# Three squares of the first batch on GpSimd, one relu more on VectorE, and the loads between them, in an attention and feed-forward kernel

## The chip, the cores and the metric

The kernel runs on one core of a Trainium2 chip. The metric is the device time of one execution in microseconds (us). The kernel before the change takes 399.31 us, the median of three runs (399.07 to 399.46).

## What is computed

The inputs are q, k and v (8 batches, 12 heads, 448 positions, 64 per head) and three weight matrices, all fp32.

```python
scores = scale * np.matmul(q, k.transpose(0, 1, 3, 2))
attn = np.maximum(scores, 0.0) ** 2 / S
x = np.matmul(attn, v)                        # then heads side by side: (3584, 768)
gate = np.maximum(x @ w_gate, 0.0)            # w_gate, w_val: (768, 1536)
out = (gate * (x @ w_val)) @ w_out            # w_out: (1536, 768)
```

So attention has no softmax: each score goes through a relu and is squared. The feed-forward part is a gated one. The kernel works in bf16 with fp32 sums and puts the scale factors into a later step.

## The kernel before, in words

**Tiles of a batch.** For each batch the scores are made in 21 tiles (`tile_of`, L244): 3 groups of four heads (`qd`) by 7 blocks of 64 positions. A tile is four matmuls that fill two PSUM banks, 128 x 896 fp32. `relu2` (L232 to L235) then takes the tile out of PSUM with a relu on ScalarE into a bf16 buffer `r_sb` (L234, from a pool of four), and squares it on VectorE into `attn` (L235). The seven squares of a group are the moving operand of 28 value matmuls (`value_passes`, L253), which add up over the seven in two other banks (banks 6 and 7, called `both`). VectorE copies their result to `x` (L663 and L669 for the first two groups; ScalarE at L685 for the third), and the two halves are swapped over partitions by `exchange` (L260; VectorE's share is L266, ScalarE's L264).

**The units of the feed-forward part.** A unit (`gv_unit`) makes 128 columns of the hidden layer of one batch in 12 steps called passes. Each pass multiplies a piece of `x` by weights from `gv_sb`, which is loaded in six chunks of 256 columns, two units each, a gate half and a value half per chunk (`load_gv`, L162 to L165).

**The order of the work.** Nothing is planned at run time. Every instruction is pinned in the order in which the program names it, so each engine's queue is as written. While batch b's attention is done, the units of batch b-1 fill TensorE. The first batch has nothing before it, and `first_batch` (L620) writes its order out by hand: tiles 0 to 16 in a loop, with relus and squares two tiles behind (`scored`, L635, takes the oldest tile from the list `todo`), then tiles 17 to 20 with the first passes of units 0, 1 and 2 among them. PSUM is short: tiles 0 to 16 take turns in three pairs of banks, so tile n can be made only when the relu of tile n-3 has read its banks. Tiles 17 and 19 take banks 2 and 3, tiles 18 and 20 banks 0 and 1; units 0, 1 and 2 add up in banks 4, 2 and 0. Ahead of it, `second_by_dve` (L638) is used once, at n = 2: VectorE does the relu of the second tile on the list (L641) and its square (L643), while the first goes through `scored`.

**The loads.** GpSimd issues nearly all loads (`dma_in`, L115), in the order of L604 to L616: k, q and v of batch 0, chunks 0 and 1 of gv, k and q of batch 1 (`load_qk(1)`, L612), and then chunks 2 and 3, v of batch 1 and chunk 4 (L613 to L616: 2 + 2 + 4 + 2 loads). After `first_batch`, at L774 to L776, it issues k of batch 2, chunk 5 and q of batch 2. GpSimd also makes copies of one element in later batches (`hold`, L703, and `hold_unit`, L699) that only wait for something and keep what stands behind them back.

Of the kernel before, what the change touches and what calls it, by code (L numbers as in the profile page):

```python
# [12 lines left out]
ALU = mybir.AluOpType  # L13
# [3 lines left out]
def kernel(  # L17
# [22 lines left out]
    nc = tc.nc  # L40
# [25 lines left out]
    HALVES = [(c, slice(c * 64, c * 64 + 64)) for c in range(2)]  # L66

    def pin(ins):
        return tc.keep_in_program_order(ins)
# [45 lines left out]
    def dma_in(o, i):  # L115
        pin(nc.gpsimd.dma_start(out=o, in_=i))  # L116
# [23 lines left out]
    def load_qk(b, h0=0, h1=H):  # L140
        load_nat(kn_b[natural(b)], k, b, h0, h1)
        load_nat(qn_b[natural(b)], q, b, h0, h1)

    def load_v(b):
        for c, p in HALVES:
            if b == 0:
                src = v[b].rearrange("(g c h) s d -> c h g s d", c=2, h=2)[c]
                dst = v_b[b % NB][p].rearrange("p (g h) i d -> p h g i d", h=2)
                parts = [(dst[:, h2], src[h2]) for h2 in range(2)]
            else:  # L150
                parts = [(v_b[b % NB][p], v[b, c * HP:c * HP + HP])]
            for dst, src in parts:
                dma_in(dst[:, :, 0:4, :], src[:, 0:256, :].rearrange("g (j i) d -> j g i d", i=4))
                dma_in(dst[:, :, 4:7, :], src[:, 256:448, :].rearrange("g (j i) d -> j g i d", i=3))
# [4 lines left out]
    gv_sb = [const.tile([128, H, n], BF16, name=f"gv{i}") for i, (_, n) in enumerate(CHUNKS)]  # L159
    wo_sb = [const.tile([128, KF // 2, d_model], BF16, name=f"wo{i}") for i in range(2)]  # L160

    def load_gv(c):  # L162
        for (_, p), src in zip(HALVES, (moe_w_gate, moe_w_val)):
            f0, n = CHUNKS[c]
            dma_in(gv_sb[c][p], src.rearrange("(h p) f -> p h f", p=64)[:, :, f0:f0 + n])  # L165

# [35 lines left out]
    def transposes(b, hp, bank):  # L202

        ps = bank.bitcast(BF16).rearrange("p (t c) -> p t c", t=2)
        for t, nat in enumerate((kn_b[b % NB], qn_b[b % NB])):
            for i in range(4):
                for h2, half in HALVES:
                    pin(nc.tensor.transpose(ps[half, t, i * 128:i * 128 + 128], nat[:, 2 * hp + h2, i, :], ident))  # L208
        pin(nc.vector.tensor_copy(T_b[b % NB][:, :, hp, :], ps[:, :, 0:S]))  # L209

    def first_transposes(numbers):

        for n, (hp, t) in zip(numbers, ((0, 0), (0, 1), (1, 0), (1, 1))):
            ps = banks[:, n, :].bitcast(BF16)
            for i in range(4):
                for h2, half in HALVES:
                    pin(nc.tensor.transpose(ps[half, i * 128:i * 128 + 128],  # L217
                                            (kn_b, qn_b)[t][0][:, 2 * hp + h2, i, :], ident))
            o = T_b[0][:, t, hp, :]
            if (hp, t) == (1, 0):  # L220
                pin(nc.scalar.activation(o, ps[:, 0:S], AF.Copy))
            else:
                pin(nc.vector.tensor_copy(o, ps[:, 0:S]))
# [5 lines left out]
                transposes(b, pair_of(b, 2 * qd + c), ps[:, c, :])  # L229
        sc_later()  # L230

    def relu2(src, dst):  # L232
        r = rpool.tile([128, 2, S], BF16, name="r_sb")
        pin(nc.scalar.activation(r, src, AF.Relu))  # L234
        pin(nc.vector.tensor_tensor(dst, r, r, ALU.mult))  # L235

    attns = {}

# [5 lines left out]
    def tile_of(b, n, ps):  # L244

        qd, i = divmod(n, NC)
        T = T_b[b % NB]
        a = i * 128 if i < 4 else (i - 4) * 128 + 64
        mm4([ps[:, r, :S] for r in range(2)], lambda r, c: T[:, 0, pair_of(b, 2 * qd + c), a:a + 64],
            lambda r, c: T[:, 1, pair_of(b, 2 * qd + c), :], True, True)  # L250
        return ps[:, :, :S], attn_of(b, qd)[:, 2 * i:2 * i + 2, :]

    def value_passes(b, qd, ps, i0, i1):  # L253

        attn, v_sb = attn_of(b, qd), v_b[b % NB]
        for i in range(i0, i1):
            mm4([ps[:, r, :S] for r in range(2)], lambda r, c: v_sb[:, 2 * qd + c, i, :],
                lambda r, c: attn[:, 2 * i + c, :], i == 0, i == NC - 1)

    def exchange(b, qd, first=None):  # L260
        x0, x1 = (x_of[b][e][qd] for e in range(2))
        for (c, p), (_, other) in zip(HALVES, HALVES[::-1]):
            if first is not None and c == 0:
                pin(first.activation(x1[p], x0[other], AF.Copy))  # L264
            else:
                pin(nc.vector.tensor_copy(x1[p], x0[other]))  # L266
# [19 lines left out]
    def idle_matmuls(ps, n):  # L286

        for _ in range(n):
            mm2(ps[:, :S], blank[:, 0:128], blank, True, True)
# [318 lines left out]
    load_nat(qn_b[0], q, 0, 8, H)  # L608
    load_v(0)
    load_gv(0)  # L610
    load_gv(1)
    load_qk(1)  # L612
    load_gv(2)  # L613
    load_gv(3)
    load_v(1)
    load_gv(4)  # L616

    NT = NQ * NC

    def first_batch(units):  # L620


        def passes(u, n):
            for _ in range(n):
                units[u].pop(0)()

        def bank(n):
            return banks[:, n, :]

        def tile(n, at=None):  # L630
            todo.append(tile_of(0, n, sc_first() if at is None else banks[:, at:at + 2, :]))

        todo = []

        def scored():  # L635
            relu2(*todo.pop(0))

        def second_by_dve():  # L638
            src, dst = todo.pop(1)
            r = rpool.tile([128, 2, S], BF16, name="r_sb")  # L640
            pin(nc.vector.tensor_scalar(r, src, 0.0, None, ALU.max))  # L641
            scored()
            pin(nc.vector.tensor_tensor(dst, r, r, ALU.mult))  # L643

        idle_matmuls(bank(6), 12)
        first_transposes((6, 7, 5, 4))
        idle_matmuls(bank(0), 4)
        tile(0)
        tile(1)
        both = banks[:, 6:8, :]  # L650
        for n in range(2, 17):
            tile(n)
            if n in (3, 5, 7, 9):
                hp = n // 2 + 1
                transposes(0, hp, bank(6 + hp % 2))
            if n == 12:
                value_passes(0, 0, both, 0, NC)
            if n == 2:
                second_by_dve()
            elif n > 3:  # L660
                scored()
            if n == 12:
                pin(nc.vector.tensor_copy(x_of[0][0][0], both[:, :, :S]))  # L663
        scored()
        value_passes(0, 1, both, 0, 4)
        passes(0, 2)
        tile(17, 2)
        value_passes(0, 1, both, 4, NC)
        pin(nc.vector.tensor_copy(x_of[0][0][1], both[:, :, :S]))  # L669
        scored()  # L670
        tile(18, 0)
        scored()
        tile(19, 2)
        passes(0, 2)
        scored()
        tile(20, 0)
        scored()
        value_passes(0, 2, both, 0, 4)
        scored()
        passes(1, 4)  # L680
        passes(2, 4)
        value_passes(0, 2, both, 4, NC)
        exchange(0, 0, nc.scalar)
        exchange(0, 1)
        pin(nc.scalar.activation(x_of[0][0][2], both[:, :, :S], AF.Copy))  # L685
        exchange(0, 2)
        for n in range(4):
            for u in range(2):
                passes(u, 2)

    def scores_event(b, n):
        return lambda: relu2(*tile_of(b, n, sc_later()))
# [77 lines left out]
    new_x(0)  # L770
    units = gv_units(0)
    first_batch(units)
    sc_later(), acc()
    load_nat(kn_b[natural(2)], k, 2, 0, H)  # L774
    load_gv(5)
    load_nat(qn_b[natural(2)], q, 2, 0, H)  # L776
    for b in range(1, B - 1):
# [8 lines left out]
        else:  # L786
            todo = [e for e in attention if e[:2] <= ENDS[b]]
# [88 lines left out]
```

## Time and profile before

| what | before |
|---|---|
| median of three runs | 399.31 us |
| the profiled execution | 399.31 us |
| its span, first to last instruction | 397.5 us |
| TensorE (PE) busy | 387.9 us, 98% |
| VectorE (DVE) busy | 302.2 us, 76% |
| ScalarE (ACT) busy | 244.3 us, 61% |
| GpSimd (POOL) busy | 97.1 us, 24% |
| granted TensorE clock | 1.000 |
| relu on ScalarE (L234) | 167 times, 936 ns each in the mean |
| square on VectorE (L235) | 167 times, 622 ns each in the mean |

The profile names engines by short names: PE is TensorE, DVE VectorE, ACT ScalarE, POOL GpSimd. A line of a timeline gives start, length, engine, line of the kernel, operation, tiles (out<-in), shapes and a count; in brackets stands how long the engine was idle before and what ended that. All starts are in us from the beginning of the span. Lengths of instructions that follow each other on an engine overlap, so the distance between two starts is the better price of one. The chain of work that ended last is followed back from the last instruction: at each step to what released it.

### The profile page before, as it was taken

What the parts mean: (1) busy time and instruction counts of PE and PEld (TensorE: products, weight loads), DVE (VectorE), ACT (ScalarE), POOL (GpSimd) and SP (SyncE); (2) the same over time, 40 slices, a digit from 0 to 9 for tenths busy, and PEclk for the clock granted to TensorE, in tenths of its full rate; (3) what the DMA queues carried; (4) which work ended last, traced back from release to release, by engine and by line L of the source; (5) the groups of instructions that cost most, each with busy time, mean ns of one, the idle gap of its engine ahead of it and who ended that gap; (6) DMA issues with size and microseconds to landing.
All of it is one profiled execution on the core that took longest, in us unless ns stands there. A gap on an engine that the chain in (4) does not pass through costs nothing.

```text
span 397.5 us, 16431 instructions
## 1 busy us (share of the span) xinstructions
PE 387.9 (98%) x7304; PEld 283.5 (71%) x7304; DVE 302.2 (76%) x531; ACT 244.3 (61%) x359; POOL 97.1 (24%) x168
## 2 busy tenths in 40 slices
PE   7899999999999999999999999999999999999995
PEld 3456679977776666666677688988887766777674
DVE  5976886689944696897873578888889869997922
ACT  3973993886334776988632788899873233444231
POOL 8933300800213601503041260020003120000213
PEclk9999999999999999999999999999999999999999
DMA  9999997999945896998963498560002340000135
GB/s 153 173 197 195 196 178 115 128 207 195 139 109 167 110 157 88 160 137 112 135 159 81 136 126 108 115 79 4 2 3 62 84 139 2 3 3 2 24 94 166
DMA packets 90872, 44.17 MB, mean 111 GB/s; under 512 B 55424, under 2 KB 89792, under 8 KB 90800
## 3 DMA queue, kind: packets, MB, share of 16 engines
q0 software_dynamic: 51264, 28.83, 51.0%
q1 hardware_dynamic: 39104, 13.99, 20.5%
q8 instruction: 57, 0.93, 1.0%
q10 hardware_dynamic: 432, 0.30, 0.3%
q14 instruction: 15, 0.12, 0.1%
HBM read 47.19 MB, written 11.01 MB: 146 GB/s over the span
## 4 chain that ended last, share of the span: by engine, by line
PE 94%; ACT 2%; DVE 1%; DMA 1%; issue 1%; POOL 0%; POOLq 0%
PE ps L72 92%; ACT r_sb L234 2%; DMA qn<-in_q_dram 1%; PE ps L208 1%; DVE attn L235 0%; DVE x L669 0%; DVE r_sb L641 0%; DVE kqT L209 0%; PE ps L217 0%; ACT g_sb L330 0%; DVE attn L643 0%; POOL qn L116 0%; DVE attn L410 0%; POOLq L860 0%
## 5 line engine op out<-in xcount | busy, mean ns | idle before, releaser
L72 PE MATMUL ps<-x,gv 64*64 64x448 bf16 (+1 forms) x3336 | 197.0, 349 | 0.1
L72 PEld LDWEIGHTS <-gv 64*64 64x64 bf16 (+1 forms) x3960 | 143.1, 107 | 48.8 <-issue 1.6
L234 ACT ACTIVATE r_sb<-ps 128x896 bf16<-128x896 f32 x167 | 148.7, 936 | 16.4 <-PE ps L72 14.0
L235 DVE TENSOR_TENSOR attn<-r_sb 128x896 bf16<-128x896 bf16 x167 | 102.0, 622 | 30.8 <-ACT r_sb L234 21.9
L420 POOL DMA_DIRECT2D out_dram<-attn x63 | 33.1, 530 | 165.1 <-DVE attn L410 130.7
L72 PEld LDWEIGHTS <-hT 128*64 128x64 bf16 x1056 | 55.9, 110 | 20.9 <-issue 1.1
L72 PE MATMUL ps<-kqT 64*64 64x448 bf16 x672 | 65.7, 351 | 2.8 <-ACT r_sb L234 2.6
L406 ACT ACTIVATE attn<-ps 128x384 f32<-128x384 f32 (+1 forms) x64 | 28.8, 450 | 64.2 <-PE ps L72 63.7
L72 PE MATMUL ps<-wo,hT 128*64 128x384 bf16 (+1 forms) x720 | 54.3, 306 | 0.0
L331 DVE TENSOR_TENSOR hT<-ps,g_sb 128x448 bf16<-128x448 f32 x72 | 44.5, 619 | 8.8 <-ACT g_sb L330 8.4
L330 ACT ACTIVATE g_sb<-ps 128x448 bf16<-128x448 f32 x72 | 39.2, 546 | 16.2 <-PE ps L72 15.9
L410 DVE TENSOR_TENSOR attn<-ps,attn 128x384 f32<-128x384 f32 (+1 forms) x48 | 22.8, 503 | 32.1 <-ACT attn L406 17.4
L72 PEld LDWEIGHTS <-vn 64*64 64x64 bf16 (+1 forms) x888 | 34.7, 107 | 11.7 <-issue 1.3
L72 PE MATMUL ps<-attn,vn 64*64 64x448 bf16 x672 | 37.1, 350 | 0.1
L72 PEld LDWEIGHTS <-kqT 64*64 64x64 bf16 x672 | 25.7, 107 | 14.2 <-issue 5.0
L539 ACT ACTIVATE kqT<-ps 128x896 f32<-128x896 f32 x18 | 16.5, 918 | 25.0 <-PE ps L72 25.0
L116 POOL DMA_DIRECT2D vn<-in_v_dram x36 | 23.7, 681 | 17.6 <-DMA wo<-in_moe_w_out_dram 11.2
L72 PE MATMUL ps<-o_ring,hT 128*64 128x384 bf16 (+1 forms) x336 | 26.0, 306 | 0.0
L706 POOL COPY flag<-kqT 128x1 bf16<-128x1 bf16 x12 | 2.7, 244 | 89.8 <-DMA kqT<-kr 68.9
L543 DVE TENSOR_TENSOR kqT<-ps,kqT 128x896 f32<-128x896 f32 x18 | 19.5, 1085 | 5.9 <-PE ps L72 4.2
L266 DVE COPY x<-x 64x896 bf16<-64x896 bf16 x33 | 13.4, 405 | 2.5 <-ACT x L685 0.7
L116 POOL DMA_DIRECT2D qn<-in_q_dram x20 | 14.7, 764 | 1.3 <-POOLq L860 0.8
(103 smaller groups left out, 289.8 us busy)
## 6 DMA issues: line engine op xcount, KB each, us to landing
out_dram<-attn POOLq DMA_DIRECT2D x48, 96.0 KB, 2.5
out_dram<-attn SPq DMA_DIRECT2D x48, 96.0 KB, 2.6
kn<-in_k_dram POOLq DMA_DIRECT2D x7, 384.0 KB, 7.4
qn<-in_q_dram POOLq DMA_DIRECT2D x7, 384.0 KB, 9.5
vn<-in_v_dram POOLq DMA_DIRECT2D x14, 192.0 KB, 9.2
gv<-in_moe_w_gate_dram POOLq DMA_DIRECT2D x6, 384.0 KB, 11.8
gv<-in_moe_w_val_dram POOLq DMA_DIRECT2D x6, 384.0 KB, 11.8
wo<-in_moe_w_out_dram POOLq DMA_DIRECT2D x2, 1152.0 KB, 14.0
```

The source lines that it names most:

```text
L72: pin(nc.tensor.matmul(o, lhsT=l, rhs=r, start=start, stop=stop, skip_group_check=True))
L116: pin(nc.gpsimd.dma_start(out=o, in_=i))
L234: pin(nc.scalar.activation(r, src, AF.Relu))
L235: pin(nc.vector.tensor_tensor(dst, r, r, ALU.mult))
L266: pin(nc.vector.tensor_copy(x1[p], x0[other]))
L330: pin(nc.scalar.activation(g_sb, o[0], AF.Relu, scale=float(out_scale)))
L331: pin(nc.vector.tensor_tensor(hT[:, mf, col:col + S], o[1], g_sb, ALU.mult))
L406: pin(nc.scalar.activation(out_of(t, r, c), bank(P, t), AF.Copy))
L410: pin(nc.vector.tensor_tensor(o, bank(Q, t), o, ALU.add))
L420: pin(engines[c].dma_start(out=rows[:, c0:c1, :], in_=src))
L539: pin(nc.scalar.activation(held(n, j), both(PQ[n][0]), AF.Copy))
L543: pin(nc.vector.tensor_tensor(k, both(PQ[n][1]), k, ALU.add))
```

## The change

In the first batch, the squares of tiles 12, 16 and 19 are made on GpSimd instead of VectorE. The relu of tile 13 is made on VectorE instead of ScalarE, by a second use of `second_by_dve` at n = 14; its own square stays on VectorE. The loop's n = 15 takes no tile from the list any more, so that the list is as long afterwards as before. The ten loads of L613 to L616 move into `first_batch`: the gate half of chunk 2 stands on GpSimd between the squares of tiles 16 and 19, the other nine behind the square of tile 19. On GpSimd the order is therefore, behind q of batch 1: square of tile 12, square of tile 16, gate half of chunk 2, square of tile 19, value half of chunk 2, chunk 3, v of batch 1, chunk 4. TensorE's order is the same as before, instruction for instruction; SP's too. VectorE's is: copy L663, square 11, relu 13, square 13, square 14, square 15, copy L669, squares 17, 18 and 20.

```diff
-    def load_gv(c):
-        for (_, p), src in zip(HALVES, (moe_w_gate, moe_w_val)):
+    def load_gv(c, parts=(0, 1)):
+        for p, src in [(HALVES[n][1], (moe_w_gate, moe_w_val)[n]) for n in parts]:
...
-    def relu2(src, dst):
+    def relu2(src, dst, square=nc.vector):
         r = rpool.tile([128, 2, S], BF16, name="r_sb")
         pin(nc.scalar.activation(r, src, AF.Relu))
-        pin(nc.vector.tensor_tensor(dst, r, r, ALU.mult))
+        pin(square.tensor_tensor(dst, r, r, ALU.mult))
...
     load_qk(1)
-    load_gv(2)
-    load_gv(3)
-    load_v(1)
-    load_gv(4)
...
-        def scored():
-            relu2(*todo.pop(0))
+        def scored(square=nc.vector):
+            relu2(*todo.pop(0), square)
 
-        def second_by_dve():
+        def second_by_dve(square=nc.vector):
             src, dst = todo.pop(1)
             r = rpool.tile([128, 2, S], BF16, name="r_sb")
             pin(nc.vector.tensor_scalar(r, src, 0.0, None, ALU.max))
-            scored()
+            scored(square)
             pin(nc.vector.tensor_tensor(dst, r, r, ALU.mult))
...
             if n == 2:
                 second_by_dve()
-            elif n > 3:
+            elif n == 14:
+                second_by_dve(nc.gpsimd)
+            elif n not in (3, 15):
                 scored()
...
         pin(nc.vector.tensor_copy(x_of[0][0][1], both[:, :, :S]))
-        scored()
+        scored(nc.gpsimd)
+        load_gv(2, (0,))
         tile(18, 0)
         scored()
         tile(19, 2)
         passes(0, 2)
         scored()
         tile(20, 0)
-        scored()
+        scored(nc.gpsimd)
+        load_gv(2, (1,))
+        load_gv(3)
+        load_v(1)
+        load_gv(4)
         value_passes(0, 2, both, 0, 4)
```

## The prediction

> **What bounds the kernel now.** I read the page first (engine shares, slices), then the chain that ended last in order of time, then the timelines of the four engines from 17 to 27 us. By the page TensorE is busy 98% of the span at full clock, and by the chain nearly all of the time after 45.81 us is TensorE work in a row. Whatever the change moves lies before that, and what TensorE loses there is lost at the end.
>
> ```profile
> 16.18 2.11 PE ps L72 x40
> ...
> 18.31 1.07 ACT r_sb L234
> ...
> 19.42 2.60 PE ps L72 x44
> ...
> 22.04 1.10 DVE x L669
> ...
> 23.18 8.62 PE ps L72 x124
> ```
>
> Columns: start, length, what. One relu of ScalarE (L234, that of tile 13) ends at 19.38 and lets TensorE go on; one VectorE copy (L669) does so again at 23.14; from 23.18 TensorE runs on its own. So the change is worth what it does to those two releases. TensorE's timeline there:
>
> ```profile
> 18.61 0.38 PE L72 MATMUL ps<-kqT 64*64 64x448 bf16 x4 [0.34 <-ACT r_sb L234]
> 19.42 0.38 PE L72 MATMUL ps<-kqT 64*64 64x448 bf16 x4 [0.43 <-ACT r_sb L234]
> 19.61 0.95 PE L72 MATMUL ps<-attn,vn 64*64 64x448 bf16 x16
> 20.36 0.72 PE L72 MATMUL ps<-x,gv 64*64 64x448 bf16 x8
> 21.04 0.38 PE L72 MATMUL ps<-kqT 64*64 64x448 bf16 x4
> 21.23 0.76 PE L72 MATMUL ps<-attn,vn 64*64 64x448 bf16 x12
> ```
>
> The lines at 18.61 and 19.42 are tiles 15 and 16: each takes the banks of the tile three before it. Tile 16 waits for tile 13's relu, **the relu that the change gives to VectorE**. Spacings to use: a tile 0.19, 16 value matmuls 0.75, 12 of them 0.57, 8 pass matmuls 0.38 where nothing is waited for. VectorE and GpSimd:
>
> ```profile
> 18.00 1.08 DVE L663 CAST x<-ps 128x896 bf16<-128x896 f32 x1
> 19.01 2.76 DVE L235 TENSOR_TENSOR attn<-r_sb 128x896 bf16<-128x896 bf16 x5
> 22.04 1.09 DVE L669 CAST x<-ps 128x896 bf16<-128x896 f32 x1 [0.28 <-PE ps L72]
> 23.04 2.76 DVE L235 TENSOR_TENSOR attn<-r_sb 128x896 bf16<-128x896 bf16 x5
> ```
> ```profile
> 18.36 0.84 POOL L116 DMA_DIRECT2D gv<-in_moe_w_gate_dram  x1
> 20.75 0.75 POOL L116 DMA_DIRECT2D gv<-in_moe_w_val_dram  x1 [1.56 <-DMA gv<-in_moe_w_val_dram]
> ```
>
> VectorE has no free slot from 18.00 to 21.76: squares follow each other every 0.535 us (0.62 each, overlapped), a copy from PSUM takes 1.0 before the next may start. The engine that is given more work is full.
>
> **The change, part by part.** *Relu of tile 13.* ScalarE loses one of its relus, which start 0.80 apart, so those of tiles 14 and 15 come 0.80 earlier. VectorE gains one: 1.09, the L641 row (8.92, same shape, same line before the change). It stands behind the copy L663 and the square of tile 11. Even if nothing disturbs these, it runs from 19.01 + 0.535 = 19.54 to 20.63, and tile 16 starts at 20.66, not 19.42: 1.24 late. Part comes back: the 8 pass matmuls at 20.36 now find their weights there (the trace ends their wait in mid-group at 20.73, on a DMA of gv) and their relus done. From tile 16 to L669 takes 0.19 + 0.75 + 0.38 + 0.19 + 0.57, with 0.2 until the last matmul is through, 2.3 against 22.04 - 19.42 = 2.62. L669 is then late by about 0.9, and with it all that follows. So the relu alone costs 0.85.
>
> *The saved relu time itself* is worth almost nothing: the passes at 20.36 wait for gv until 20.73 whatever ScalarE does, and L669 hangs on them.
>
> *Three squares to GpSimd (tiles 12, 16, 19).* VectorE gives up 3 x 0.535. The trace has no such square on GpSimd. Below: 1.2, from the one-element flag copy (0.19) and the 128-element AFFINE_SELECT (0.33), by (0.33 - 0.19) x 7 + 0.19. Above: 7 x 0.33 = 2.3. VectorE's own 0.62 is a floor for both. I take **2.0**, nearer to the upper end, because a square reads two operands and AFFINE_SELECT one. The Trainium skill, GPSIMD Engine Reference, section "Performance versus the Vector engine", gives 4497 ns for a tensor_tensor of 2048 fp32 elements; scaled to 896 this is an estimate of 1.97, and the sum would be the same.
>
> *Do they run beside VectorE's squares?* This trace has rows:
>
> ```profile
> 228.18 0.63 DVE L235 TENSOR_TENSOR attn<-r_sb 128x896 bf16<-128x896 bf16 x1
> ```
> ```profile
> 228.30 0.55 POOL L701 COPY flag<-hT 128x1 bf16<-128x1 bf16 x1 [6.16 <-DVE hT L331]
> ```
> ```profile
> 130.86 0.67 DVE L235 TENSOR_TENSOR attn<-r_sb 128x896 bf16<-128x896 bf16 x1 [0.29 <-ACT r_sb L234]
> ```
> ```profile
> 130.75 0.30 POOL L706 COPY flag<-kqT 128x1 bf16<-128x1 bf16 x2
> ```
> ```profile
> 260.92 0.19 POOL L706 COPY flag<-kqT 128x1 bf16<-128x1 bf16 x1 [5.62 <-DMA kqT<-qr]
> ```
>
> A GpSimd copy of one element takes 0.19 beside a VectorE operation that reads PSUM (260.92). Begun inside a VectorE square it lasts until just past the square's end (228.30 + 0.55 against 228.18 + 0.63). Begun before one, at 130.75, it is not held, and the square is 0.04 longer than the usual 0.62 to 0.63. So a square and a GpSimd read exclude each other, and who is first goes first. I take that for the long squares too: **each GpSimd square stops VectorE's squares for its whole 2.0 us.** The Trainium skill, SBUF — State Buffer, section "Who interferes with whom", states it as a rule that speaks against this change: a VectorE instruction with two SBUF inputs and a GpSimd instruction that reads SBUF block each other for a whole instruction. By that rule the sum is the one that follows, without it the 0.85 above; the flag rows agree with it, most clearly in one direction.
>
> The sum, in order of time:
> 1. Tile 12's relu ends at 18.56; GpSimd is free (its last load ended at 18.45) and squares from 18.60 to 20.60. VectorE is in L663, from PSUM, so GpSimd is first.
> 2. Behind L663, tile 11's square waits until 20.60 and ends near 21.15. Queued behind it is tile 13's relu, 21.1 to 22.2, and for that waits TensorE: tile 16 at 22.2, **2.8 late**.
> 3. TensorE needs 2.3 to L669, which starts at 24.5 (before: 22.04) and ends at 25.6.
> 4. Tile 16's square holds GpSimd and the port from 23.95 to 25.95, mostly beside L669; tile 17's ends at 26.5. Tile 20 runs at 26.0, the first 16 value matmuls at 26.2, the 32 pass matmuls at 26.95 to 28.46 (1.5 as before).
> 5. GpSimd issues one load (0.75, to 26.70), then wants tile 19's square (relu done 26.6), meets tile 18's square on VectorE until 27.07, and works from 27.1 to 29.1. Tile 20's relu is done at 27.46, but its square waits until 29.1 and ends at 29.68.
> 6. The last 12 value matmuls: tile 18 at 28.46, tile 19 at 29.13, tile 20 at 29.71, the last issued by 29.90. Before, they began at 26.02 and were issued by 26.61: **+3.3**.
> 7. The half-swap copies L266 on VectorE, before at 25.83, now follow tile 20's square and end 0.1 behind TensorE: +0.1. TensorE's wait for qn at 32.21 shrinks by 0.06.
>
> In all +3.3. With 1.2 for a square the same steps give +1.6, with 2.31 +4.2.
>
> *The ten loads that move* (gv2, gv3, v1, gv4) and those queued behind them on GpSimd (kn, gv5, qn, first at 38.52) I cost at nothing. Each issue before waits for an older landing (20.75 above); landings come some 2 us apart, and qn of batch 1, the last load ahead of the moved ones, lands at 32.36. The moved ones now start at 25.95, 29.1 and 29.9, still ahead of that. Without this cover gv2 would be 2 us later per load; its user, unit 4, starts at 36.8 + 3.3, so 3 us of that are covered too. SP's queue is not touched.
>
> **The rivals.** (a) *No mutual hold*: VectorE's squares run beside GpSimd's. Then only the relu counts: +0.85 - 0.06, 400.1. For it: the holds seen last 0.4 at most. (b) *GpSimd always gives way*: its first square then ends at 22.9 instead of 20.6, 0.55 after the value matmuls want it; with the relu's 0.85 that is +1.4 by L669, and the later two add up to 1.5: 400.7 to 402.2. For it: the clear flag rows are all of this direction; against it, 130.86. (c) *Not slower*: there is no hold, and the 0.85 is swallowed further on. TensorE's load queue has waits of 0.4, 0.2, 0.3 and 0.4 near 45, 53, 80 and 91 us; if what ends them does not move with TensorE, they take it all: 399.3. It decides from 0.85 of such time on. Against it: the chain names L234 relus and L330 there, which follow TensorE's own tiles. (d) *Faster*: VectorE gets to tile 13's relu before 18.3; then ScalarE's 0.80 counts, but the gv landing at 20.73 leaves some 0.1: 399.2. The full VectorE row speaks against it.
>
> **How the numbers follow.** The profiled execution took 399.31 us (span 397.5, 1.8 around it), equal to the median 399.31 of three runs. Forecast: 399.31 + 3.3 = 402.6, chance 0.65, its own range 400.9 (1.2 per square) to 403.6 (2.31). (b) 0.10, (a) 0.15, (c) 0.07, (d) 0.03. The range reaches down to (a) and up to the price's upper end: 400.0 to 403.7. A change of 0.2%, 0.8 us, is about what a measurement of this kernel can tell from none; (a) lies on that bound and is split in two. Slower 0.83, same 0.14, faster 0.03.
>
> **What would show it.** GpSimd squares of 1.2 to 2.3 us at about 18.6, 24 and 27; a VectorE square begun at 19.0 that lasts some 2 us; tile 16 at 22.2, its wait ended by VectorE's relu (L637); L669 (now L667) at 24.5; the last value matmuls of the first batch at 28.5 to 30; unit 4's weights without a wait. It is wrong if the VectorE squares beside GpSimd's keep their 0.62 (then tile 16 is at 20.7), if a GpSimd square takes under 1 us, or if TensorE waits for gv after 36 us.

## The result, and the profile after

The changed kernel takes 403.54 us, the median of six runs (402.93 to 404.21), against 399.76 us for the kernel before (six runs, 399.07 to 401.48): ratio 1.0091, 95% interval 1.0072 to 1.011, so slower by 0.9%. The profiled execution has a span of 401.7 us (before 397.5). Forecast were 402.6 us and +3.3; the medians differ by 3.8, the two profiled spans by 4.2. Two of all the executions below, at a mean clock of 0.75 (512.78 us) and 0.56 (683.91 us), ran slow throughout and count in no ratio. A ratio is the recorded one; it can differ by up to 0.0012 from the quotient of the medians beside it.

The chain that ended last, in the changed kernel (start, length, what):

```profile
18.88 1.86 DVE attn L235
20.73 1.01 DVE r_sb L637
...
21.79 3.87 PE ps L72 x34
...
25.68 1.10 DVE x L667
```

Where the chain before had one relu of ScalarE, it now has a VectorE square of 1.86 us and VectorE's relu behind it; only then does TensorE go on, at 21.79. The copy of the second group (now L667) follows at 25.68, before at 22.04. The timelines of GpSimd and VectorE in the changed kernel:

```profile
18.57 1.68 POOL L235 TENSOR_TENSOR attn<-r_sb 128x896 bf16<-128x896 bf16 x1
23.48 1.68 POOL L235 TENSOR_TENSOR attn<-r_sb 128x896 bf16<-128x896 bf16 x1 [3.23 <-ACT r_sb L234]
25.10 0.80 POOL L116 DMA_DIRECT2D gv<-in_moe_w_gate_dram  x1
27.67 1.71 POOL L235 TENSOR_TENSOR attn<-r_sb 128x896 bf16<-128x896 bf16 x1 [1.77 <-ACT r_sb L234]
```
```profile
18.88 1.86 DVE L235 TENSOR_TENSOR attn<-r_sb 128x896 bf16<-128x896 bf16 x1
20.66 1.08 DVE L637 TENSOR_SCALAR r_sb<-ps 128x896 bf16<-128x896 f32 x1
28.64 1.22 DVE L235 TENSOR_TENSOR attn<-r_sb 128x896 bf16<-128x896 bf16 x1 [0.80 <-ACT r_sb L234]
29.89 3.25 DVE L266 COPY x<-x 64x896 bf16<-64x896 bf16 x5
```

A GpSimd square takes 1.68. A VectorE square that comes up while one runs (18.88, 28.64) ends 0.48 after it, though alone it takes 0.62 (GpSimd's ends at 18.57 + 1.68 = 20.25, VectorE's at 20.74). This is the hold of which the prediction speaks. TensorE's timeline:

```profile
21.79 0.59 PE L72 MATMUL ps<-kqT 64*64 64x448 bf16 x4 [2.86 <-DVE r_sb L637]
22.11 1.75 PE L72 MATMUL ps<-attn,vn 64*64 64x448 bf16 x16
...
31.88 1.31 PE L72 MATMUL ps<-x,gv 64*128 64x448 bf16 x12 [0.40 <-DVE x L266]
```

The 16 value matmuls that took 0.95 now take 1.75, and there is a new wait of 0.40 for the swap copies (`exchange`, L266, five on VectorE in this stretch). The reason of the first stands in the busy time by stretches (us, busy time and count of each engine, granted TensorE clock, DMA share, GB/s), for the changed kernel:

```profile
18.90:21.60 2.70, 0.03 (x3) 0.00 (x0) 2.70 (x3) 1.17 (x2) 1.36 (x1) 1.00 1.47 202
21.60:25.00 3.40, 3.21 (x36) 2.01 (x39) 1.83 (x4) 1.06 (x2) 1.52 (x1) 0.50 1.44 193
```

From 21.60 to 25.00 **the granted clock is 0.50**: after 2.7 us without work TensorE runs at half speed just when it is let go. In a table, with the time of each mark (us):

| mark | before | forecast | after | late by |
|---|---|---|---|---|
| tile 16 starts | 19.42 | 22.2 | 21.79 | 2.37 |
| copy of the second group starts | 22.04 | 24.5 | 25.68 | 3.64 |
| last 12 value matmuls start | 26.02 | 28.46 | 29.66 | 3.64 |
| batch 1's transposes start | 31.73 | | 36.12 | 4.39 |
| first value matmuls of batch 1 | 45.81 | | 49.95 | 4.14 |

From there to the end nothing more is lost. The next link of the chain, before and after, is as long in both, and the span is 4.2 longer:

```profile
45.81 46.05 PE ps L72 x958
```
```profile
49.95 46.04 PE ps L72 x958
```

This led to a theory of three parts, which the experiments test: (1) the GpSimd square holds VectorE's, and the relu queued behind makes TensorE wait; (2) that wait lowers TensorE's clock; (3) the loads, issued in a burst, hold the swap copies. The rivals: the relu's late place alone; GpSimd's squares alone; the third square's hold, as predicted; slow matmuls for another reason.

### The profile page after: what moved, and what is told of

It reads as the page before. It is cut to its first block, busy times and chain, and to the rows that moved or that the text cites. A ratio compares the mean times of both kernels' runs of the same rounds, so it can differ in the third digit from the quotient of the medians.

```text
span 401.7 us, 16433 instructions
## 1 busy us (share of the span) xinstructions
PE 389.3 (97%) x7304; PEld 281.6 (70%) x7304; DVE 304.9 (76%) x529; ACT 244.2 (61%) x358; POOL 102.0 (25%) x171
## 4 chain that ended last, share of the span: by engine, by line
PE 91%; DVE 4%; ACT 1%; DMA 1%; issue 1%; POOL 1%; POOLq 0%; ACTq 0%
PE ps L72 90%; DVE attn L235 2%; ACT r_sb L234 1%; DMA qn<-in_q_dram 1%; PE ps L208 1%; DVE kqT L209 1%; DVE x L266 0%; POOL qn L116 0%; POOL kn L116 0%; DVE x L667 0%; DVE r_sb L637 0%; DVE attn L410 0%; ACT g_sb L330 0%; POOL ident L112 0%; POOLq L112 0%
## 5 line engine op out<-in xcount | busy, mean ns | idle before, releaser
L72 PE MATMUL ps<-attn,vn 64*64 64x448 bf16 x672 | 38.1, 355 | 0.1
L266 DVE COPY x<-x 64x896 bf16<-64x896 bf16 x33 | 14.6, 443 | 1.8
```

The costliest lines, as they stand in the source:

```text
L72: pin(nc.tensor.matmul(o, lhsT=l, rhs=r, start=start, stop=stop, skip_group_check=True))
```

## The experiments

### The relu alone

```diff
+            elif n == 14:
+                second_by_dve()
-            elif n > 3:
+            elif n not in (3, 15):
                 scored()
```

This is the kernel before with that edit; squares and loads stay. It was run twice.

> The relu of tile 13 on VectorE, as in the change; all squares on VectorE and all loads where they were before. Theory (the GpSimd square holds VectorE's square, and the relu queued behind it makes TensorE wait): without a GpSimd square the VectorE square of tile 11 keeps 0.62 us, the relu starts at 19.5, tile 16 at 20.7, and TensorE's wait is too short for its clock to fall: span +0.8 us against the kernel before. Rival (VectorE's late place for the relu is the whole cost, GpSimd's squares are harmless): +4 us, as in the changed kernel.

> The relu of tile 13 on VectorE and nothing else, once more, for a profile at full clock. In the first set its executions lay between 397.9 and 401.1 us of span, the long ones at a mean granted clock of 0.993 to 0.995, the short ones at 1.000. Theory: the relu itself costs 0.8 us (tile 16 at 20.7, span 398.3); what lies above that in the median is the clock, which falls for 3.4 us in those executions in which TensorE's waits of 1.1 to 1.9 us fall together in one window: the profile shows either 1.00 throughout and some 398.3, or a stretch at 0.50 and 399.5 to 400.5. Rival (the relu costs 1.7 us without the clock): 399.2 or more at a clock of 1.00 throughout.

First set: 401.46 against 399.58 (eleven executions), ratio 1.0042 (1.0025 to 1.006); no times are read from its trace. Second set: 400.81 against 399.52, ratio 1.0022 (1.0 to 1.0044), profiled span 397.9 at full clock. VectorE and TensorE in that one:

```profile
18.73 0.61 DVE L235 TENSOR_TENSOR attn<-r_sb 128x896 bf16<-128x896 bf16 x1
19.26 1.08 DVE L641 TENSOR_SCALAR r_sb<-ps 128x896 bf16<-128x896 f32 x1
```
```profile
20.39 0.38 PE L72 MATMUL ps<-kqT 64*64 64x448 bf16 x4 [1.62 <-DVE r_sb L641]
```

With no GpSimd square the square of tile 11 keeps 0.61, tile 16 is 0.97 late instead of 2.37, and the copy of the second group starts at 22.72, 0.68 late. This run began 0.22 earlier (its tile 15 at 18.39, before 18.61): counted from tile 15, tile 16 is 1.19 late and the copy 0.90, close to the prediction's 1.24 and 0.9. The span is 0.4 longer, 0.6 when counted in the same way; the rest is made up at batch 1's transposes (0.25, below). The rival with +4 us falls. The scatter is large: in the second set seven executions of 397.9 to 399.1 us of span at a mean clock of 0.998 or more, five of 399.9 to 400.8 at 0.994 or 0.995. In the first set five of eleven are at 0.993 to 0.995; one of 400.8 at 0.999 doesn't fit and stays open. The expectation that the clock falls in some executions fits the split; the profile caught one without a fall, so a fall in this kernel is read from the mean clock alone.

### The relu alone, with TensorE kept busy

Beside the edit above, eight idle steps of two matmuls each stand ahead of tile 16:

```diff
         for n in range(2, 17):
+            if n == 16:
+                idle_matmuls(bank(6), 8)
             tile(n)
```

> The relu of tile 13 on VectorE alone, and 16 idle matmuls on zeros into banks 6 and 7 ahead of tile 16, overwritten later, so that TensorE works through its wait. Theory (clock): the executions no longer scatter, the clock stays at 1.00, and the span is 398.3, 0.8 us above the kernel before: the price of the relu's place alone. Rival (the scatter has nothing to do with TensorE's wait): the median stays 1.7 us above the kernel before.

400.08 against 399.52, ratio 1.0004 (0.9984 to 1.0024). Ten of twelve spans lie between 398.0 and 398.7, none with a mean clock under 0.997; two are longer (399.5, which is the profiled one, and 399.8) at full clock. In the profiled one TensorE stands for 1.01 us at 177.73 with nothing in the profile that it waits for, far behind the change; without that it would have 398.5. Filling the wait takes the group of long executions away. What remains, 0.56 between the medians, is the price of the relu's place, and some of it is the filling's own: tile 16 comes 2.16 behind tile 15 here, against 2.00 without the idle matmuls.

### GpSimd's squares and the moved loads, without the relu

```diff
-            elif n == 14:
-                second_by_dve(nc.gpsimd)
-            elif n not in (3, 15):
-                scored()
+            elif n > 3:
+                scored(nc.gpsimd if n == 14 else nc.vector)
```

> The squares of tiles 12, 16 and 19 on GpSimd and the loads behind them, as in the change; the relu of tile 13 stays on ScalarE. Theory (hold): tile 16 at 19.4 as before; the VectorE square of tile 11 lasts some 1.9 us, ScalarE's relu of tile 15 waits for its buffer until 20.7, tile 17 comes 0.8 us late, and with the third hold and the slower swap copies the span grows by 1.0 to 1.6 us; no fall of the clock, since no wait of TensorE is much over 1 us. Rival (the relu is the whole cost): 0. Rival (the squares are the whole cost, wherever the relu is): +4 us.

401.41 against 399.58, ratio 1.0048 (1.0036 to 1.006), span 399.4 with the clock at 1.00 throughout. TensorE's timeline in this kernel:

```profile
19.42 0.38 PE L72 MATMUL ps<-kqT 64*64 64x448 bf16 x4 [0.43 <-ACT r_sb L234]
21.86 0.38 PE L72 MATMUL ps<-kqT 64*64 64x448 bf16 x4 [0.93 <-ACT r_sb L234]
```

Tile 16 is on time, since its relu is not behind the held square. Tile 17 is 0.8 late by a way that the prediction had not named: the held square of tile 11 keeps its r_sb buffer, and ScalarE's relu of tile 15 waits 0.72 for that and starts at 20.90. With the third hold and the swap copies the span is 1.9 longer, somewhat over the 1.0 to 1.6 expected; both rivals (0 and +4) fall. In the profiled spans squares and relu cost 1.9 and 0.6 apart and 4.2 together: the relu makes the hold worse (it stands behind it), and only together is TensorE's wait long enough for the clock to fall in most executions (nine of twelve, by the mean clock in two sets).

### The changed kernel, with TensorE kept busy

Tile 16 of the changed kernel gets the idle matmuls of the second experiment ahead of it, with 13 instead of 8: 26 matmuls.

> The changed kernel with 26 idle matmuls on zeros into banks 6 and 7 ahead of tile 16, so that TensorE works through its wait of 2.9 us; their result is overwritten. Theory (the wait lets the granted clock fall to 0.50 for 3.4 us, which costs about 1.6 us): the clock stays at 1.00, from tile 16 to the copy L667 takes 2.3 us instead of 3.9, span 400.1, 1.6 us less than the changed kernel. Rival (TensorE is slow there for another reason, operands or loads): the slow spacing stays and the span is 401.7 or more.

401.78 against 399.58, ratio 1.0059 (1.0046 to 1.0072); span 399.8, all five between 399.8 and 400.5. TensorE's timeline, and the busy time by stretches:

```profile
18.73 2.65 PE L72 MATMUL ps<-blank 128*64 128x448 bf16 x26
21.45 0.38 PE L72 MATMUL ps<-kqT 64*64 64x448 bf16 x4
```
```profile
21.40:23.80 2.40, 2.35 (x48) 1.69 (x49) 1.73 (x4) 1.52 (x3) 0.66 (x1) 1.00 1.44 193
```

The clock stays at 1.00, and from tile 16 to the copy of the second group takes 23.77 - 21.45 = 2.32 instead of 3.89. Useless work makes the changed kernel 1.9 us faster in the span; 0.3 of that is that this run began earlier (its tile 15 at 18.20, in the changed kernel 18.54), and **1.6 us were the clock**. The medians say the same: 2.2 above the kernel before, where the changed kernel is 3.8 above. The rival (slow for another reason) falls.

### The third square back on VectorE

```diff
         tile(20, 0)
-        scored(nc.gpsimd)
+        scored()
```

> The changed kernel with the square of tile 19 on VectorE again; GpSimd keeps tiles 12 and 16. Theory (the loads issued in a burst behind the third GpSimd square slow the VectorE copies L266 that swap halves, 0.42 to 0.74 us instead of 0.39, and that costs 0.5 us): the burst comes 3.4 us earlier, the copies take 0.39 again but for one, span 401.2, 0.5 us less than the changed kernel; tile 16 still at 21.8 and the clock still falls. Rival (the third square's hold has the price that the prediction gave it, 0.8 us): 0.8 less or more. Rival (neither costs): 401.7.

402.24 against 399.58, ratio 1.0071 (1.0058 to 1.0083), span 400.5. The span is 1.2 shorter than that of the changed kernel, which by the bounds set beforehand would speak for the rival. But the clock's fall lies 1.5 us later here (23.12 to 26.54) and partly over a wait, so tile 16 to the copy takes 3.27 instead of 3.89; that is 0.6 of the 1.2. The stretch behind the copy of the second group can be compared. The chain that ended last, of this kernel and then of the changed one:

```profile
26.36 8.68 PE ps L72 x122
```
```profile
26.82 0.79 PE ps L72 x12
...
31.88 4.32 PE ps L72 x43
36.19 2.80 PE ps L208 x96
```

From that copy to the transposes TensorE needs 8.69 here (26.36 to 35.05; before 23.18 to 31.80, 8.62) and 9.37 in the changed kernel. The 0.68 are what the third square and the burst cost together. The last value matmuls of the changed kernel are as late as the copy (3.64 both), so the hold did not delay them. It reaches TensorE only through the swap copies, which stand behind the held square (it ends at 29.86, they begin at 29.89) and are slow besides. This run changes both, since without the third square the loads are issued earlier too.

### The loads held until the swap copies are done

```diff
-        load_gv(2, (1,))
-        load_gv(3)
-        load_v(1)
-        load_gv(4)
...
         exchange(0, 1)
+        pin(nc.gpsimd.tensor_copy(flag[:, 3:4], x_of[0][1][1][:, 1, S - 1:S]))
+        load_gv(2, (1,))
+        load_gv(3)
+        load_v(1)
+        load_gv(4)
```

> The changed kernel, with the nine loads behind the square of tile 19 held back by a one-element copy on GpSimd that waits for the second pair of swap copies (L266); tile 19's square stays on GpSimd. Theory (the burst of load issues slows the swap copies): the first copies take 0.39 us instead of 0.42 to 0.74, TensorE's wait of 0.4 at 31.9 goes, and 0.5 to 0.7 us of the changed kernel's time goes with it: span 401.0 to 401.2; the held weights still land before unit 4 wants them. Rival (the copies are slow because of the third GpSimd square ahead of them): the copies stay slow and the span stays at 401.7. Rival (the held loads come too late): TensorE waits for gv past 36 us and the span grows.

402.61 against 399.52, ratio 1.0075 (1.0052 to 1.0099); the profiled span is 401.5, and the twelve scatter from 399.4 to 402.5, too much to decide by. The timeline of VectorE decides. The swap copies in the kernel before, then this kernel:

```profile
25.83 1.23 DVE L266 COPY x<-x 64x896 bf16<-64x896 bf16 x3
```

```profile
28.46 1.37 DVE L235 TENSOR_TENSOR attn<-r_sb 128x896 bf16<-128x896 bf16 x1 [0.80 <-ACT r_sb L234]
29.87 1.23 DVE L266 COPY x<-x 64x896 bf16<-64x896 bf16 x3
```

The third GpSimd square is still there and still holds a VectorE square (1.37), but the first three swap copies take 1.23, as before the change, where the changed kernel needs 1.94 for them (29.89 to 31.83 in its chain). The chain from the copy of the second group to the transposes is 8.82 instead of 9.37:

```profile
26.64 8.82 PE ps L72 x124
```

So it is the burst of load issues that slows the copies, 0.55 of the 0.68; the other 0.13 would be the hold's. No wait for the held weights shows. The expected 0.5 less is there when batch 1's first value matmuls start (49.22 instead of 49.95), but about as much is lost again near 228 us, where the chain of this run has 4.52 us of an output DMA. What that has to do with the edit, if anything, is not shown.

### The relu ahead of the held square

```diff
+        def by_dve_ahead():
+            (s11, d11), (s13, d13) = todo.pop(0), todo.pop(1)
+            r11 = rpool.tile([128, 2, S], BF16, name="r_sb")
+            pin(nc.scalar.activation(r11, s11, AF.Relu))
+            r13 = o_ring.rearrange("p n m -> p (n m)")[:, 0:S].bitcast(BF16).rearrange("p (r s) -> p r s", r=2)
+            pin(nc.vector.tensor_scalar(r13, s13, 0.0, None, ALU.max))
+            pin(nc.vector.tensor_tensor(d11, r11, r11, ALU.mult))
+            return lambda: pin(nc.vector.tensor_tensor(d13, r13, r13, ALU.mult))
...
-            elif n == 14:
-                second_by_dve(nc.gpsimd)
+            elif n == 13:
+                square13 = by_dve_ahead()
+            elif n == 14:
+                scored(nc.gpsimd)
+                square13()
```

> The changed kernel with VectorE's relu of tile 13 ahead of the square of tile 11 instead of behind it, its result in a free piece of another buffer so that the four r_sb buffers keep their turn; all three squares stay on GpSimd and the loads behind them. Theory (a GpSimd square holds a VectorE instruction with two SBUF inputs, not one that reads PSUM): the relu keeps 1.09 us beside the GpSimd square of tile 12 and ends at 20.0, tile 16 at 20.0, the square of tile 11 behind it still waits for the end of GpSimd's; TensorE's wait is 1.2 us, the clock stays up, and with the slower swap copies the span is 398.2 to 398.8. Rival (GpSimd slows whatever VectorE does): the relu is held until 20.3 and ends at 21.3 or later, span 400 or more.

400.48 against 399.52, ratio 1.0015 (0.9996 to 1.0034), span 398.7, clock 1.00. GpSimd's and VectorE's timelines:

```profile
18.60 1.68 POOL L235 TENSOR_TENSOR attn<-r_sb 128x896 bf16<-128x896 bf16 x1 [0.15 <-ACT r_sb L234]
21.85 2.06 POOL L235 TENSOR_TENSOR attn<-r_sb 128x896 bf16<-128x896 bf16 x1 [1.57 <-ACT r_sb L234]
```
```profile
18.91 1.08 DVE L646 TENSOR_SCALAR o_ring<-ps 128x896 bf16<-128x896 f32 x1
19.90 0.86 DVE L647 TENSOR_TENSOR attn<-r_sb 128x896 bf16<-128x896 bf16 x1
21.22 1.15 DVE L235 TENSOR_TENSOR attn<-r_sb 128x896 bf16<-128x896 bf16 x2
```

As expected. The relu, which reads PSUM, runs its full length beside GpSimd's square without delay (1.08); the square after it, which reads r_sb, is held until GpSimd is done. The other direction shows too: GpSimd's second square, issued at 21.85 inside a VectorE square that ends at 22.37, takes 2.06 instead of 1.68. The rival falls. With the same work in another order (and the relu's result in another buffer) the changed kernel loses 3 us of its span, of which the clock is about 1.6; what is left above the kernel before is the swap copies (TensorE again waits 0.40 for them) and the hold of tile 20's square.

### The same, with the third square on VectorE and two passes moved

Beside the edit above: tile 19's square back, and `passes(0, 2)` of unit 0 behind the value matmuls of the second group instead of ahead of tile 17.

> The kernel with VectorE's relu of tile 13 ahead of the square of tile 11, the squares of tiles 12 and 16 on GpSimd, that of tile 19 on VectorE again, and the first two passes of unit 0 moved behind the value matmuls of the second group, where TensorE waits for a copy anyway. Theory: nothing is held that TensorE waits for; tile 16 at 20.0, the copy of the second group at 21.9 to 22.1 (before 22.04), no burst beside the swap copies, the clock stays up: span 397.3 to 397.6, the same as the kernel before, and not less, since TensorE's wait for batch 1's qn near 32.2 is set by the loads. Rival (GpSimd's squares cost by themselves): 398.5 or more.

399.8 against 399.41, ratio 1.0002 (0.9979 to 1.0025), profiled span 398.1: the same as the kernel before, as expected, though the profiled span is 0.5 above the expected window. Tile 16 comes at 20.35 and the copy of the second group at 22.54, both some 0.4 later than expected. Of this 0.2 is that the run began later (tile 15 at 18.81, before 18.61), and two of the swap copies still meet load issues (0.67 and 0.63 us). In this order two GpSimd squares can be had for nothing, but nothing is won by them either.

### The changed kernel again

> The changed kernel as it is, beside the kernel before on the chip of this set. Theory: a fall of the granted clock to 0.50 for 3.4 us in all or nearly all executions, since TensorE waits 2.9 us for tile 16 in each; span 400.5 to 402 by where the fall lies, median 1.0 to 1.2% above the kernel before. Rival (the fall is rare, as in the kernel with the relu alone): a scatter down to 399.8, the span of the kernel that keeps TensorE busy.

403.33 against 399.41, ratio 1.0086 (1.0054 to 1.0118). Four of six executions have a mean clock of 0.993 to 0.996 and spans of 400.9 to 402.9, two have 0.998 and 399.9 and 400.5. So the fall comes in most executions but not in all: the expectation "all or nearly all" was too strong, and the ratio is under the 1.0 to 1.2% expected. The two others are as long as the kernel that keeps TensorE busy. In the first set one of six had 0.998 too, with a span of 401.1; why it is longer than these two stays open.

## Why the prediction was right, and where its terms were not

The direction and the range held, and so did the mechanism that the prediction named, the hold. But the largest cost after it, 1.6 us of half clock, was not in the sum, and that the forecast came within 0.9 of the span is in part luck: for a GpSimd square of 1.68 the prediction's own +1.6 (at 1.2) and +3.3 (at 2.0) give some +2.6, and a square taken too long and a third hold that never came hid about 1.3 of the 2.2 that were missing (the clock and the swap copies). (A small slip beside it: +4.2 on 399.31 is 403.5, not 403.6.)

- **The hold** (steps 1 and 2) is shown. The VectorE square behind GpSimd's takes 1.86 with the relu behind it (changed kernel), 0.61 without GpSimd's square, and the relu set ahead of it is not held. The flag copies of 0.19 and 0.55 us had told it. The Trainium skill's rule in SBUF — State Buffer, "Who interferes with whom", agrees in every part seen here (SBUF is the memory of all tiles that are not in PSUM): two SBUF inputs block and are blocked (1.86; 2.06 for 1.68), a PSUM input doesn't (1.08).
- **The GpSimd square** was taken as 2.0 and measured 1.68, inside the bounds of 1.2 to 2.3. Tile 16 was therefore 2.37 late, not 2.8.
- **Step 3 failed.** "TensorE needs 2.3 to L669" assumed full speed; it needed 3.89, at half the clock. The step looked at what TensorE waits for and not at what waiting does to it. With TensorE kept busy the 2.32 is there. The Trainium skill, TensorE: Matmul & The Clock Gate, "Part 1: The HAM clock gate", tells of free-running windows of 3413 ns after which the clock is set anew; here the half clock lasts 21.596 to 25.009, 3.413 us, and starts 17.067 us, five such windows, after the first clock record of the trace. The Trainium skill speaks there of an idle window; this one, from 18.18, still held 0.40 us of matmuls. The traces say how much is too little. Columns as in the stretches above; TensorE's busy time is the third number, and the lines are the window before the fall in the changed kernel, the same in `square19_back`, and the emptiest one of the relu alone (second set), after which no fall came:

```profile
18.18:21.60 3.41, 0.40 (x7) 0.11 (x4) 3.41 (x3) 1.89 (x3) 1.94 (x2) 1.00 1.46 201
```
```profile
19.71:23.12 3.41, 1.17 (x28) 0.90 (x30) 3.38 (x5) 1.39 (x2) 0.71 (x1) 1.00 1.45 198
```
```profile
18.48:21.90 3.42, 1.80 (x36) 1.18 (x39) 3.42 (x7) 2.51 (x3) 1.31 (x2) 1.00 1.46 200
```

Counted in such windows from the first clock record of each profile (all but the first of the relu alone), every window with 1.17 us of TensorE work or less is followed by half clock, also at the very end of a run, and none with 1.68 us or more is. So where the windows happen to lie against TensorE's wait would decide whether an execution escapes. That is read from the traces; no experiment moved the windows.

- **Steps 5 and 6 failed** in size: the third square was to add 0.8 by 29.9, and to the value matmuls it added nothing. From the copy of the second group to the last 12 is 3.98 in the changed kernel as before, and these take 0.77; so it is at full clock too, in `kept_busy` (27.75 - 23.77). Where TensorE waits less for tile 16, in `squares_alone` and `relu_first`, the 12 take 1.00 and 1.04, so there the third hold costs some 0.25.
- **Step 7** was mis-sized: the swap copies were to cost 0.1 and cost 0.7, most of it by the burst. The ten loads were costed at nothing because their landings are not late, and they are not: TensorE has no wait for gv after 36 us. But issuing them is work on GpSimd too, and it meets VectorE copies that read and write SBUF: 0.39 us each before, 3.25 for five after.
- **Batch 1's qn**, the load that the second group of its transposes needs: the wait at 32.21 was taken as 0.06. These groups follow each other every 0.22 and the gap was 0.48 (31.73 to 32.21), so the wait was 0.25, and that much is taken off whatever comes late. It also lowers the price of the relu alone: 0.68 at the copy, 0.4 at the end.
- **The terms together**: 2.37 for tile 16, +1.57 clock, -0.30 regained behind tile 16 (2.62 to 2.32), +0.75 swap copies, -0.25 at qn: 4.14, as the mark at 45.81 says.
- **The rivals.** (a), no hold, is out; its price for the relu alone was 0.8, and 0.6 was measured, counted from tile 15. (b), GpSimd always gives way, is out by the held VectorE squares. (c) counted on later waits near 45, 53, 80 and 91 us: from 45.81 to the end 4.14 stays 4.2, so they move along with TensorE. (d) asked that VectorE begin the relu before 18.3; it never did (20.66 in the changed kernel, 18.91 where it was set first), and setting it first brought no gain over the kernel before.

## What to carry to other kernels

Before work is moved to an engine that looks idle, ask whether it can run at the same time as what the busy engine does then: here a GpSimd elementwise operation kept VectorE's two-operand squares out until it was done, so each 0.54 us that VectorE was to be spared could cost it 1.2 us of standing still (0.62 became 1.86). What is queued behind the held instruction decides the price; setting one PSUM-reading relu ahead of it gave 3 us of span back. Look also at the granted clock behind a new TensorE wait: here a wait of 2.86 us cost 1.6 us more at half speed, and idle matmuls over the wait took that back. And count the issues of moved loads as work on their engine, beside the copies that the other engine makes then.

## What the runs showed of the hardware that was not expected

- After TensorE had waited 2.86 us its granted clock was 0.50 for 3.41 us, which cost 1.57 us more. Waits of 1.6 us (the relu alone) went with a mean clock of 0.994 or 0.995 in five of twelve executions. In windows of 3.413 us, the fall came after 0.40, 0.44, 0.87 and 1.17 us of matmuls and did not come after 1.68 us or more.
- Back-to-back load issues on GpSimd (0.69 to 0.79 us each) stretched VectorE's SBUF-to-SBUF bf16 copies (64x896) from 0.39 us to between 0.42 and 0.74, while the issues themselves grew by some 0.05.
- A 128x896 bf16 square, both operands the same SBUF tile, takes 1.68 us on GpSimd and 0.62 on VectorE.
